# Weight words of the attention stage: one staging buffer against two, and reads one or two slots ahead against three

## The chip, the cores and the metric

The kernel runs on one core of a Trainium2 chip. The metric is the device time of one execution in microseconds (us). Three executions of the kernel before took 984.76, 985.96 and 990.31 us; the median, 985.96, stands for it below.

## The reference

A causal attention with a bias made of running sums (4 batches, 8 heads, 576 positions, 64 wide) is followed by two feed-forward blocks of 2304 tokens, 512 wide inside and 2048 wide in the middle:

```
x = attention(q, k, v, s)                     # 2304 x 512
g = relu(x @ moe_w_in) ** 2                   # 2304 x 2048
y = g @ moe_w_out                             # 2304 x 512
h = y @ moe2_w_in                             # 2304 x 2048
out = max(0.01 * h, h) @ moe2_w_out           # 2304 x 512
```

The four weight matrices arrive as 64-bit words, so the kernel has to read 8 bytes for each weight and build a 32-bit float from the low and the high half.

## The kernel before, in words

**Stages.** The first stage does attention and, in between, the first product of the first block (`up1`). A tail without attention follows, with the last token blocks of `up1`; then come `down`, `up` and `down` again for the other three products. The change lies in the first stage, function `attention`.

**Slots.** Attention runs over 16 pairs of heads, 7 slots each (`n = len(STEPS)`), so `end` is 112. In each slot one row tile of scores is reduced on VectorE (line 438), goes through the exponential on ScalarE (line 462, nine instructions for a pair) and is turned on TensorE two slots later (line 472). The products with `v` are line 508. From slot 39 on `fill` mixes matmuls of `up1` (line 593) into the slots: block `j` of 512 tokens starts behind slot `START[j] = 28 * (j + 1) + 10`, and its 16 groups, one for each chunk of `moe_w_in`, are spread over the 23 slots behind that. Each group ends with a Relu (line 579) and a Square (line 580) on ScalarE.

**Weights in attention.** Sixteen jobs `load_w` make the chunks of `moe_w_in` that `up1` multiplies with, two and a half slots apart from slot `CV` on. Thirteen jobs `convert` (`BEFORE`) make chunks of `moe_w_out`, three slots apart from slot 72 on, and write them to a scratch in HBM (line 180). A job is a generator; `at_slot` says in which slots it goes one step on. One chunk is 128 x 512 words of 64 bits, 512 KB.

- The read is line 153 (`moe_w_in`) or line 151 (`moe_w_out`), on SP's queue, into a tile `wst`.
- `words` builds the floats: line 112 (ScalarE, high words to `wt`), line 116 (VectorE, shift), line 118 or 114 (ScalarE, low words in place), line 120 (the addition: GpSimd for `moe_w_in`, VectorE for `moe_w_out`), line 121 (VectorE, sign; the last use of `wst`).
- `load_w` then splits the result: line 166 (VectorE, copy) and line 167 (GpSimd, subtraction).

Line 112 stands one slot behind the read in `load_w`, two slots behind it in `convert`. `Stage(mx, mx, 1)` gives `wst` one buffer in the pool `mx`, so the read of a chunk waits for line 121 of the chunk before it.

**Other work of GpSimd in a pair:** the low parts of q and k (line 394), small copies of the last rows (line 402), the widened sums (line 531).

**Order.** Each engine runs its instructions in a fixed order. Where a job's step is asked for in a slot, the scheduler of the language still sorts all instructions by when it takes them to be ready, with the program's order as the priority. A change of one dependency can so move many instructions on all engines.

Of the kernel before, what the change touches and what calls it, by code (L numbers as in the profile page):

```python
# [18 lines left out]
def f32(ap):  # L19
    return ap.bitcast(F32)  # L20
# [3 lines left out]
def attention_then_two_mlps(  # L24
# [24 lines left out]
    nc = tc.nc  # L49
# [8 lines left out]
    NR1 = S - R  # L58
    W = 512
    LAG = 2  # L60
    CV = 13
    SB, HN = 768, 384
    ORDER = (1, 7, 6, 2, 5, 4, 3)
    CHAIN = {1: 0, 6: 0, 5: 0, 3: 0, 7: 1, 4: 1, 2: 2}
# [15 lines left out]
    wpool = first.enter_context(tc.tile_pool(name="w", bufs=1))  # L80
# [28 lines left out]
    def words(t, st, adder=nc.gpsimd):  # L109

        lw, hw = st[:, :, 0], st[:, :, 1]
        nc.scalar.activation(f32(t), f32(hw), AF.Copy, scale=2.0 ** -112)  # L112
        if adder is nc.vector:
            nc.scalar.activation(lw, lw, AF.Copy, scale=2.0 ** -29)  # L114
            yield
        nc.vector.tensor_scalar(t, t, 0x07FFFFFF, 3, ALU.bitwise_and, ALU.logical_shift_left)  # L116
        if adder is not nc.vector:
            nc.scalar.activation(lw, lw, AF.Copy, scale=2.0 ** -29)
            yield
        adder.tensor_tensor(t, t, lw, ALU.add)  # L120
        nc.vector.scalar_tensor_tensor(t, hw, 0xC0000000, t, ALU.bitwise_and, ALU.bitwise_or)  # L121
        yield
# [25 lines left out]
    def read_w(st, w, ch, rows, queue=nc.sync):  # L148

        if rows:  # L150
            queue.dma_start(st.rearrange("p f t -> p (f t)"), w.bitcast(U32)[ch * P:(ch + 1) * P, :])
        else:
            queue.dma_start(
                st.rearrange("p (c f) t -> p c (f t)", c=KC),
                w.bitcast(U32)[:, ch * 2 * P:(ch + 1) * 2 * P].rearrange("(c p) f -> p c f", p=P))

    def load_w(fc, pool, stage, lo_engine=nc.gpsimd):

        st = stage.words()
        read_w(st, w1_in, fc, False)  # L160
        yield
        dst = pool.tile([P, 2, DM], F32R, tag=f"w{fc}", name=f"w{fc}")
        win[fc] = dst
        t = stage.word()
        yield from words(t, st)
        nc.vector.tensor_copy(dst[:, 0], f32(t))
        lo_engine.tensor_tensor(dst[:, 1], f32(t), f32(dst[:, 0]), ALU.subtract)
# [3 lines left out]
    def convert(mat, ch, stage, queue=nc.gpsimd, lag=3):  # L171

        w, rows = LATER[mat]
        st = stage.words()
        read_w(st, w, ch, rows, queue)
        for _ in range(lag):
            yield
        t = stage.word()
        yield from words(t, st, nc.vector)
        nc.gpsimd.dma_start(wscr[mat][ch], f32(t))  # L180
# [379 lines left out]
    def up1_x(mp, j, c, bufs):  # L560

        n, w = BLOCKS[j]
        xf = mp.tile([P, w], F32, tag="xf", name="xh", bufs=2)
        nc.sync.dma_start(xf, xscr[c, :, n:n + w])
        yield
        t = mp.tile([P, 2, w], F32R, tag="xs", name="xs", bufs=bufs)
        xs[j, c] = t
        split([t[:, z] for z in range(2)], xf)
# [32 lines left out]
    def attention(at, mg, mx):  # L601
# [5 lines left out]
        def at_slot(y, f, *args):  # L607
            later.setdefault(y, []).append((f, args))
# [52 lines left out]
        def store(x):  # L661
            p = pairs[x]
            for e in range(2):
                c, d0 = divmod(p.h[e] * D, P)
                nc.sync.dma_start(xscr[c, d0:d0 + D, p.b * S:(p.b + 1) * S], p.xo[64 * e:64 * e + 64])

        for fc in range(FC):
            job = load_w(fc, wpool, Stage(mx, mx, 1))
            for gap in range(4):
                at_slot(CV + 5 * fc // 2 + gap, step, job)  # L670
        for ch in range(BEFORE):
            job = convert(0, ch, Stage(mx, mx, 1), nc.sync, 2)
            for gap in (0, 1, 2, 3, 4, 5):
                at_slot(end - 3 * BEFORE - 1 + 3 * ch + gap, step, job)
        START = [4 * n * (j + 1) + 10 for j in range(B)]
        for j in range(B):
            for c in range(KC):
                job = up1_x(mx, j, c, XS)
# [295 lines left out]
    with tc.tile_pool(name="mg", bufs=1) as mg, tc.tile_pool(name="mx", bufs=1) as mx:  # L974
        with tc.tile_pool(name="at", bufs=1) as at:
            attention(at, mg, mx)
        pad, wr = [late.enter_context(tc.tile_pool(name=x, bufs=1, side="right", reuse_waits="tile"))
                   for x in ("pd", "wr")]
        pad.tile([P, 120], F32, tag="pad", name="pad")
        for i in EARLY:  # L980
            wparts[i] = wr
        with tc.tile_pool(name="s3", bufs=1, side="right", reuse_waits="tile") as s3,                 tc.tile_pool(name="s2", bufs=1, side="right", reuse_waits="tile") as s2,                 tc.tile_pool(name="mt", bufs=1, side="right", reuse_waits="tile") as mt:
            stage, other = Stage(s2, s2, 2), Stage(s3, s3, 1)
            for x in range(BEFORE, BEFORE + 7):
                jobs.add(x - BEFORE, convert, *divmod(x, FC), stage, nc.gpsimd, 2)
            for at, q, x in ((0, 0, other), (5, 1, other), (10, 2, other), (12, 3, stage)):
                jobs.add(at, arrive, 0, q, x, EARLY, True)
            for c in range(KC):
                for _ in up1_x(mt, B, c, KC):
                    pass  # L990
            for j in (B - 1, B):
                for _ in up1(mg, j, jobs.tick):
                    pass
            jobs.finish()
# [6 lines left out]
    with ExitStack() as stack:  # L1001
        b = open_pools(stack, ("b10", "bp2", "bp1", "bwst", "b00", "b01", "bop0", "bop1", "b11", "bwt"))
        stage = Stage(b["bwst"], b["bwt"], 2)
# [10 lines left out]
    with ExitStack() as stack:  # L1014
        b = open_pools(stack, ("c62", "cpa", "cpb", "cwst", "c17", "cy", "c543", "cp2", "cwa", "cwt"))
        stage, other = Stage(b["cwst"], b["cwt"], 2), Stage(b["cwa"], b["cwa"], 6)
# [52 lines left out]
```

## Time and profile before

| | |
|---|---|
| median of three executions | 985.96 us |
| the profiled execution | 989.75 us |
| its span, first to last instruction | 986.9 us |
| mean granted clock of TensorE | 0.989 of full speed |
| busy: TensorE, its weight loads | 942.2, 840.5 us |
| busy: VectorE, ScalarE, GpSimd | 691.5, 595.0, 203.0 us |
| DMA moved | 178.5 MB, 181 GB/s |

The span is 2.85 us shorter than the profiled execution's time. In the rows PE is TensorE, PEld its weight loads, DVE VectorE, ACT ScalarE, POOL GpSimd, SPq SP's queue of DMAs, and L112 line 112. Busy shares are means over the whole span, and the stages differ: attention with its `up1` takes about the first 350 us, the tail goes to about 450 us, and the other three products take the rest. Matmuls are pipelined and their ends are modelled, so a busy TensorE is not one at its peak. An idle time is put down to the event that ended it.

### The profile page before, as it was taken

The numbers are of one execution on the slowest core, as the hardware profiler recorded it, in microseconds if no ns is written. First come the engines' busy times: TensorE is split into PE (matmuls) and PEld (weight loads), VectorE is DVE, ScalarE is ACT, GpSimd is POOL, SyncE is SP. The second block draws the span as 40 slices with busy tenths as digits, with TensorE's granted clock in tenths as the row PEclk, the third lists the DMA queues.
The fourth block names the chain that finished last, engine by engine and source line by source line (L and its number), as shares of the span: only waits on it lengthen the run. The fifth ranks groups of instructions, "written<-read, shape, count | busy, mean of one in ns | idle before, by whom it ended". The sixth has DMA issues, their size and how long they took to land.

```text
span 986.9 us, 16713 instructions
## 1 busy us (share of the span) xinstructions
PE 942.2 (95%) x6056; PEld 840.5 (85%) x6056; DVE 691.5 (70%) x1281; ACT 595.0 (60%) x1095; POOL 203.0 (21%) x329
## 2 busy tenths in 40 slices
PE   5998999899999999889999999999999999999998
PEld 4665766677767768789999999999999999999998
DVE  6787667644585534648889799679568788685863
ACT  5775766665667646766566556568567764444442
POOL 5565555422232002100121100101111000000000
PEclk9998999999999999999999999999999999999999
DMA  8774756473754565994856833866868674617201
GB/s 143 142 169 111 183 170 143 128 187 103 204 161 153 172 204 195 323 345 149 273 179 204 295 102 113 258 204 231 319 199 301 206 257 122 183 42 221 75 17 49
DMA packets 191818, 178.50 MB, mean 181 GB/s; under 512 B 101428, under 2 KB 167028, under 8 KB 191736
## 3 DMA queue, kind: packets, MB, share of 16 engines
q1 hardware_dynamic: 153712, 98.35, 36.1%
q0 software_dynamic: 11776, 41.03, 12.2%
q10 hardware_dynamic: 26248, 38.06, 10.5%
q8 instruction: 47, 0.77, 0.3%
q14 instruction: 35, 0.29, 0.1%
HBM read 111.25 MB, written 66.13 MB: 180 GB/s over the span
## 4 chain that ended last, share of the span: by engine, by line
PE 38%; DMA 9%; issue 7%; DVE 6%; ACT 3%; POOL 1%; SPq 0%; ACTq 0%; POOLq 0%; DVEq 0%
PE q L773 36%; DVE op L879 3%; DMA gp<-gscr 2%; DMA wst<-in_moe_w_in_dram 2%; PE h L593 2%; DMA gscr<-gs 1%; DMA wst<-in_moe_w_out_dram 1%; DVE gp L873 1%; DMA xh<-xscr 1%; DMA wb<-wscr 1%; DMA gp<-qscr 1%; ACT r L579 1%; ACT op L878 0%; ACT wst L114 0%; DVE gp L871 0%
## 5 line engine op out<-in xcount | busy, mean ns | idle before, releaser
L773 PE MATMUL q<-op,w 128*128 128x384 f32 x2016 | 354.9, 336 | 7.3 <-DVE op L879 4.7
L773 PEld LDWEIGHTS q<-op,w 128*128 128x128 f32 x2016 | 350.5, 188 | 11.6 <-DVE op L879 6.8
L878 ACT ACTIVATE op<-gp 128x768 fp32r<-128x768 f32 x189 | 158.1, 845 | 160.9 <-PE q L773 138.6
L593 PE MATMUL h<-xs,w 128*128 128x512 f32 (+1 forms) x960 | 224.7, 382 | 6.7 <-ACT r L579 3.7
L879 DVE TENSOR_TENSOR op<-gp,op 128x768 fp32r<-128x768 f32 x189 | 178.1, 955 | 47.5 <-ACT op L878 47.3
L593 PEld LDWEIGHTS h<-xs,w 128*128 128x128 f32 x960 | 162.3, 190 | 43.3 <-ACT r L579 6.5
L773 PE MATMUL q<-w,op 128*128 128x256 f32 x1512 | 182.1, 283 | 1.0 <-DVE op L879 1.0
L773 PEld LDWEIGHTS q<-w,op 128*128 128x128 f32 x1512 | 181.7, 192 | 1.4 <-DVE op L879 1.4
L462 ACT ACTIVATE t<-t,m 128x128 f32<-128x128 f32 (+2 forms) x144 | 83.3, 580 | 43.0 <-DVE m L438 40.9
L438 DVE CUSTOM_DVE_ANT_0 t<-S,mask 128x128 f32<-128x128 f32 (+2 forms) x129 | 57.9, 475 | 39.6 <-PE S L422 22.9
L472 PE MATMUL tr<-ident,t 128*128 128x128 f32 x384 | 68.0, 288 | 11.9 <-ACT t L462 11.1
L180 POOL DMA_DIRECT2D wscr<-wt x48 | 26.7, 556 | 245.2 <-DVE wt L121 231.6
L472 PEld LDWEIGHTS tr<-ident,t 128*128 128x128 f32 x384 | 45.8, 144 | 30.7 <-ACT t L462 14.2
L112 ACT ACTIVATE wt<-wst 128x512 f32<-128x512 f32 x64 | 42.4, 662 | 45.1 <-DMA wst<-in_moe_w_in_dram 24.1
L579 ACT ACTIVATE r<-h 128x512 f32<-128x512 f32 (+1 forms) x80 | 43.6, 547 | 33.2 <-PE h L593 32.6
L848 DVE TENSOR_TENSOR post<-q,post 128x768 f32<-128x768 f32 x54 | 51.6, 955 | 15.2 <-PE q L773 14.8
L508 PE MATMUL tr<-pT,v 128*64 128x320 f32 (+3 forms) x384 | 54.6, 404 | 3.9 <-DVE pT L718 3.8
L116 DVE TENSOR_SCALAR wt<-wt 128x512 uint32<-128x512 uint32 x64 | 30.2, 472 | 39.4 <-ACT wt L112 39.3
L718 DVE COPY pT<-tr 128x384 f32<-128x384 f32 (+2 forms) x80 | 40.4, 521 | 22.9 <-PE tr L472 22.9
L121 DVE SCALAR_TENSOR_TENSOR wt<-wst,wt 128x512 uint32<-128x512 uint32 x64 | 48.5, 757 | 11.0 <-POOL wt L120 10.2
L422 PE MATMUL S<-Y 64*128 64x128 f32 (+3 forms) x354 | 44.3, 358 | 9.4 <-ACT Y L393 9.3
L508 PEld LDWEIGHTS tr<-pT,v 128*64 128x64 f32 x384 | 29.5, 142 | 27.4 <-DVE pT L718 6.7
(103 smaller groups left out, 1025.8 us busy)
## 6 DMA issues: line engine op xcount, KB each, us to landing
gscr<-gs ACTq DMA_DIRECT2D x36, 512.0 KB
gp<-gscr SPq DMA_DIRECT2D x48, 384.0 KB
qscr<-post ACTq DMA_DIRECT2D x48, 384.0 KB
gp<-qscr SPq DMA_DIRECT2D x48, 384.0 KB
wscr<-wt POOLq DMA_DIRECT2D x48, 256.0 KB, 4.5
wst<-in_moe_w_out_dram POOLq DMA_DIRECT2D x19, 512.0 KB, 5.4
wst<-in_moe_w_in_dram SPq DMA_DIRECT2D x16, 512.0 KB
wst<-in_moe_w_in_dram POOLq DMA_DIRECT2D x16, 512.0 KB, 5.6
```

The lines of the kernel that those rows point to most:

```text
L121: nc.vector.scalar_tensor_tensor(t, hw, 0xC0000000, t, ALU.bitwise_and, ALU.bitwise_or)
L422: nc.tensor.matmul(p.sc[kind][e][:, a:z], qs[hs, T * P:(T + 1) * P], ks[hs, :z - a], start=(n == 0 and y == 0), stop=(n == len(tiles) - 1 ...
L438: return nc.vector.tensor_tensor_reduce(t[:, a:z], sc, msk, -QK_SCALE, first, ALU.add, ALU.min, m).ins
L462: done = nc.scalar.activation(t[:, a:z], t[:, a:z], AF.Exp, bias=m[:, c:c + 1], scale=-1.0, accum_out=sums[:, s0:s0 + 1])
L472: nc.tensor.transpose(tr[:, c * P:(c + 1) * P], t[:, c * P:(c + 1) * P], ident)
L508: p.anchor = nc.tensor.matmul(po[64 * e:64 * e + 64, a:n], p.vr[:, c, e], rhs[e], start=(y == 0), stop=(y == len(mm) - 1), skip_group_chec ...
L579: nc.scalar.activation(r[:, :w], h[:, :w], AF.Relu)
L593: nc.tensor.matmul(h[:, :w], win[fc][:, a, c * P:(c + 1) * P], xs[j, c][:, z, :w], start=(c == 0 and y == 0), stop=(c == KC - 1 and y == 2))
L773: i = nc.tensor.matmul(*args, skip_group_check=True, **kw).ins
L848: done = nc.vector.tensor_tensor(t[1], acc, t[1], ALU.add)
L878: a = nc.scalar.activation(t[:, 0], src, AF.Copy)
L879: c = nc.vector.tensor_tensor(t[:, 1], src, f32(t[:, 0]), ALU.subtract)
```

## The change

It alters five things, all in `attention` or the job that it calls.

- `wst` and `wt` of the attention stage move from pool `mx`, which lives on through the tail, to pool `at`, which is freed at the end of attention. `wst` gets two buffers instead of one; `wt` keeps two.
- In `load_w` line 112 stands three slots behind the read instead of one; the job takes six slots instead of four.
- `CV`, the slot of the first read, is 11 instead of 13. The first line 112 stays in slot 14.
- In `convert` as attention uses it line 112 stands three slots behind the read instead of two. The slots of the reads stay, so each conversion comes one slot later.
- `BEFORE` stays 13.

```
-    CV = 13
+    CV = 11
...
         read_w(st, w1_in, fc, False)
-        yield
+        for _ in range(3):
+            yield
         dst = pool.tile([P, 2, DM], F32R, tag=f"w{fc}", name=f"w{fc}")
...
+        stage = Stage(at, at, 2)
         for fc in range(FC):
-            job = load_w(fc, wpool, Stage(mx, mx, 1))
-            for gap in range(4):
+            job = load_w(fc, wpool, stage)
+            for gap in range(6):
                 at_slot(CV + 5 * fc // 2 + gap, step, job)
         for ch in range(BEFORE):
-            job = convert(0, ch, Stage(mx, mx, 1), nc.sync, 2)
-            for gap in (0, 1, 2, 3, 4, 5):
+            job = convert(0, ch, stage, nc.sync, 3)
+            for gap in range(6):
                 at_slot(end - 3 * BEFORE - 1 + 3 * ch + gap, step, job)
```

In the changed kernel the lines behind 161 have numbers that are higher by one, those behind 668 by two.

Two places show what the scheduler makes of it. The first is SP's queue of DMAs in the second pair; `v` and `ag` are the values and the bias rows of a coming pair. Before:

```order
L370 DMA v<-in_v_dram 128x4x64
L382 DMA ag_88<-aug 4x1152 x2
L370 DMA v<-in_v_dram 128x4x64
L372 DMA v<-in_v_dram 64x2x64
L153 DMA wst<-in_moe_w_in_dram 128x4x256
L370 DMA v<-in_v_dram 128x4x64 x2
L372 DMA v<-in_v_dram 64x2x64
L382 DMA ag_90<-aug 4x1152 x2
```

Now:

```order
L153 DMA wst<-in_moe_w_in_dram 128x4x256
L383 DMA ag_88<-aug 4x1152 x2
L371 DMA v<-in_v_dram 128x4x64 x2
L373 DMA v<-in_v_dram 64x2x64
L153 DMA wst<-in_moe_w_in_dram 128x4x256
L371 DMA v<-in_v_dram 128x4x64 x2
L373 DMA v<-in_v_dram 64x2x64
L383 DMA ag_90<-aug 4x1152 x2
```

The read of the first chunk now stands ahead of the bias rows of one pair and the values of another, where the second chunk's read takes its old place.

The second place is VectorE in the third pair, ahead of all `up1` work; `t,m<-S,mask` is the reduction of the scores, `w` a finished chunk. Before:

```order
L121 SCALAR_TENSOR_TENSOR wt<-wst,wt 128x512
L523 TENSOR_SCALAR sums<-sums 128x4
L166 CAST w_569<-wt 128x512
L524 RECIPROCAL sums<-sums 128x4
L438 ISA t,m<-S,mask 128x512
L438 ISA m 128x1
L718 COPY pT_683<-tr 128x3x128
L438 ISA t,m<-S,mask 128x512
```

Now:

```order
L121 SCALAR_TENSOR_TENSOR wt<-wst,wt 128x512
L524 TENSOR_SCALAR sums<-sums 128x4
L116 TENSOR_SCALAR wt<-wt 128x512
L167 CAST w_571<-wt 128x512
L525 RECIPROCAL sums<-sums 128x4
L439 ISA t,m<-S,mask 128x512
L439 ISA m 128x1
L121 SCALAR_TENSOR_TENSOR wt<-wst,wt 128x512
```

One conversion stood between these reductions, two stand there now: line 116 of the next chunk and its line 121 came in between. Over the stage the conversions move up as a whole. Ahead of the 52nd exponential on ScalarE stood six instructions of line 112, now nine; line 112 of the sixteenth chunk stood behind 85 exponentials, now behind 67; and the Square of the sixteenth `up1` group stood behind 90, now behind 79.

## Rows read from the trace of the kernel before

**Rows 1.** The chain that ended last: its first step; start us, us, what.

```profile
354.36 0.02 SPq L665
```

**Rows 2.** Windows: us; busy PE, PEld, DVE, ACT, POOL; PE's clock, DMA share, GB/s.

```profile
75.00:100.00 25.00, 21.76 (x128) 14.50 (x125) 18.95 (x54) 15.22 (x39) 13.20 (x19) 0.86 0.41 108
125.00:150.00 25.00, 24.20 (x157) 17.81 (x157) 15.54 (x45) 17.25 (x41) 13.47 (x17) 1.00 0.50 159
150.00:175.00 25.00, 22.87 (x143) 16.88 (x142) 18.05 (x52) 15.39 (x37) 11.87 (x17) 0.93 0.67 155
175.00:200.00 25.00, 21.72 (x145) 16.43 (x144) 17.31 (x51) 16.19 (x37) 11.46 (x18) 0.93 0.39 114
200.00:225.00 25.00, 25.00 (x142) 18.72 (x141) 10.60 (x32) 17.10 (x41) 5.30 (x11) 1.00 0.76 189
275.00:300.00 25.00, 22.71 (x150) 16.74 (x150) 19.91 (x57) 17.47 (x44) 8.05 (x13) 1.00 0.53 162
```

**Rows 3.** Waits in the first 360 us: total, times, longest.

```profile
ACT wt L112 <- DMA wst<-in_moe_w_in_dram: 19.5, 14, 3.4
ACT wt L112 <- DMA wst<-in_moe_w_out_dram: 14.4, 8, 4.3
DVE wt L121 <- POOL wt L120: 10.2, 8, 1.8
```

**Rows 4.** TensorE's timeline: idle gaps behind a conversion; idle and releaser in brackets.

```profile
52.76 0.66 PE L472 MATMUL tr<-ident,t 128*128 128x128 f32 x4 [1.93 <-ACT t L462]
82.93 1.12 PE L472 MATMUL tr<-ident,t 128*128 128x128 f32 x4 [2.10 <-ACT t L462]
136.19 0.74 PE L593 MATMUL h<-xs,w 128*128 128x512 f32 x2 [0.31 <-DVE w L166]
151.58 0.73 PE L593 MATMUL h<-xs,w 128*128 128x512 f32 x2 [1.14 <-DVE w L166]
179.56 0.33 PE L472 MATMUL tr<-ident,t 128*128 128x128 f32 x1 [2.91 <-ACT t L462]
276.45 0.66 PE L472 MATMUL tr<-ident,t 128*128 128x128 f32 x4 [0.68 <-ACT t L462]
295.15 0.66 PE L472 MATMUL tr<-ident,t 128*128 128x128 f32 x4 [1.60 <-ACT t L462]
```

**Rows 5.** Timeline: a read on SP's queue and three of line 112 that waited for reads.

```profile
75.72 0.40 SPq L153 DMA_DIRECT2D wst<-in_moe_w_in_dram  x1
50.73 0.66 ACT L112 ACTIVATE wt<-wst 128x512 f32<-128x512 f32 x1 [2.46 <-DMA wst<-in_moe_w_in_dram]
80.91 0.66 ACT L112 ACTIVATE wt<-wst 128x512 f32<-128x512 f32 x1 [3.40 <-DMA wst<-in_moe_w_in_dram]
293.18 0.66 ACT L112 ACTIVATE wt<-wst 128x512 f32<-128x512 f32 x1 [4.30 <-DMA wst<-in_moe_w_out_dram]
```

**Rows 6.** Instructions of a conversion: ns min/median/max; last, issue of a read to landing.

```profile
L116 DVE TENSOR_SCALAR wt<-wt x16: 384/428/1596, 38.8 to 185.4; 128x512 uint32<-128x512 uint32 x16
L120 POOL TENSOR_TENSOR wt<-wt,wst x16: 1277/1302/1326, 39.3 to 187.1; 128x512 uint32<-128x512 uint32 x16
L121 DVE SCALAR_TENSOR_TENSOR wt<-wst,wt x15: 642/693/1896, 42.9 to 178.9; 128x512 uint32<-128x512 uint32 x15
L166 DVE CAST w<-wt x15: 385/428/1064, 44.0 to 182.2; 128x512 fp32r<-128x512 f32 x15
L167 POOL TENSOR_TENSOR w<-wt,w x16: 1270/1282/1300, 45.1 to 191.7; 128x512 fp32r<-128x512 f32 x16
DMA to landing us min/median/max: 3.9/5.4/9.0
```

**Rows 7.** Windows, columns as in rows 2: the second and the fourth pair, and pairs two to five.

```profile
24.00:38.00 14.00, 12.08 (x101) 9.00 (x99) 9.81 (x37) 9.79 (x27) 5.54 (x13) 1.00 0.66 150
52.60:65.80 13.20, 12.77 (x93) 8.54 (x93) 11.87 (x40) 9.91 (x30) 9.48 (x17) 0.87 0.49 132
24.00:83.80 59.80, 52.22 (x402) 37.60 (x401) 49.86 (x166) 42.64 (x114) 33.92 (x55) 0.96 0.71 156
```

## Prediction

> **What bounds the kernel now.** I begin with the chain of waits, and it does not help: followed back from the end it reaches only to 354 us [rows 1], so it never enters attention. What it shows of waits for `wst` belongs to the tail, whose staging buffers the change does not touch. Attention has to be read from the windows, the waits and the timeline.
>
> The windows say where TensorE is short of work [rows 2]. From 200 to 225 us it is busy for all 25 us at full clock while VectorE is busy for 10.6: there attention is bound by TensorE, and a wait elsewhere costs nothing. In five other windows it has idle time: 3.24 us (75 to 100), 0.80 (125 to 150), 2.13 (150 to 175), 3.28 (175 to 200) and 2.29 (275 to 300), together 11.74 us. In three of these the granted clock is below 1 as well, 0.86, 0.93 and 0.93. The two levels are 2.4 and 1.2 GHz, so a mean of 0.86 is 28% of 25 us at the lower one, 7 us in which half the work is done: 3.5 us lost. The two windows at 0.93 lose 1.75 us each. Idle time and clock make 18.7 us, which is the most that any repair between 75 and 350 us can return.
>
> The waits name a suspect [rows 3]: line 112, the first step of a conversion, waited for its read 22 times, 33.9 us in all. A read issued at 75.72 us let line 112 start at 80.91, 5.2 us later [rows 5]; the reads of GpSimd's queue took 5.4 us in the median and up to 9.0 [rows 6]. A slot early in attention is 2 us long (14.0 us for a pair of seven slots [rows 7]), so a lead of one slot cannot cover such a read. ScalarE runs in order, hence the exponentials behind line 112 wait too, and TensorE behind them: its gap of 2.10 us at 82.93 stands two us behind the wait of 3.40, the gap of 1.60 at 295.15 behind the wait of 4.30 [rows 4, 5].
>
> **The change part by part.**
>
> *Earlier reads and two buffers.* Three slots are 6 us at 14 us a pair, more than 5.2, though less than the slowest 9.0. The twelve pairs behind the fourth share the time from 65.8 to some 354 us [rows 1, 7], 24 us each, so three slots are some 10 us there, enough for all. I take the waits of rows 3 for reads as gone. What that is worth goes by TensorE alone. Of its gaps between 75 and 350 us six end on an exponential or a weight behind a conversion [rows 4]: 2.10 + 0.31 + 1.14 + 2.91 + 0.68 + 1.60 = 8.74 us, 74% of the 11.74. With the same share of the clock's 7.0 us, 5.2, that is 13.9. Not all of it comes back, since a conversion also waits inside itself, VectorE at line 121 for GpSimd's line 120, 10.2 us in 8 times [rows 3], and nothing takes that away. I keep three quarters: **-10 us**. The bounds are -3.7 (only the two gaps that follow a long read wait directly, 2.10 and 1.60) and -18.7 (all of it).
>
> *Conversions that move up.* The order shows nine of line 112 ahead of the 52nd exponential where six stood. So three conversions leave the stretch that TensorE bounds and enter the one where attention runs almost alone, bound by its own chain. Each brings VectorE 0.43 + 0.69 + 0.43 = 1.55 us at the medians [rows 6], 4.65 for three. A pair with only the start of one conversion took 14.0 us with VectorE busy for 9.81; one with more took 13.2 with 11.87 busy [rows 7]. There is room, but not for all: 1.3 us free in the fuller pair. Against it stands the gap of 1.93 us at 52.76 [rows 4], which goes with the read wait of 2.46 us ahead of it [rows 5]. I take +4.65 - 1.93, about **+3 us**; the bounds are -2 (all fits, the gap goes) and +19 (worked out below, with the slower rival).
>
> *SP's queue.* The first read moves ahead of one pair's `ag` and `v` loads. SP's issue of such a read takes 0.40 us [rows 5], 29 reads as before. A read now waits for the line 121 of two chunks earlier, and it stands one slot behind that step; loads of `q`, `k` and `v` queued behind it wait along, as they did behind the read of one chunk earlier. Nothing added: 0.
>
> *Conversions of `moe_w_out` one slot later, and `wst` in pool `at`.* The scratch writes come a slot later, long before the tail reads them. Taking `wst` out of `mx` moves every tile of `at` down by 8 KB, so the first reads of the tail wait for other tiles of the last pair than before. Last uses in the last pair differ by a slot or so. I take 0; below a shorter wait of one slot, above a longer one, 3.4 us at 24 us a pair, either way.
>
> *Everything resorted.* The scheduler moved instructions on all engines up to the end of attention and a few at the start of the first `down`. The work is the same. I price this at nothing and leave it in the width of the range.
>
> The sum: -10 + 3 = **-7 us**. The profiled execution took 989.75 us, so its counterpart is 982.75. It lies 3.8 us above the median of the three executions, 985.96, and the time that I give is for the median: 985.96 - 7 = **979.0 us**, 0.7% faster. A measurement of this kernel can tell about 0.5% from no change, 4.9 us here: faster is under 981.0, slower over 990.9.
>
> **The rivals.**
>
> *Slower: VectorE and GpSimd cannot carry the conversions where they now stand.* Nine conversions over the 3.7 pairs of exponentials 18 to 51 are 2.4 a pair. VectorE needs 9.81 + 2.4 x 1.55 = 13.5 us for a pair, still under 14.0. But line 121 also waits for GpSimd, 1.3 us a time in rows 3, which makes 16.7; and line 121 has taken 1896 ns where its median is 693 [rows 6], about the length of one GpSimd addition, 1302 ns, longer. If each conversion meets both, a pair takes 19.8 us. Pairs two to five took 59.8 us [rows 7]; at 19.8 they take 79, +19, and with the -10 of later the kernel ends at 985.96 + 9 = 995. It decides where these pairs go over 17.5 us each: 2.5 more than their mean of 15.0, four times, is the gain. For it speaks that GpSimd, busy for 9.48 of 13.2 us in the fuller pair [rows 7], gets 2.58 us more with each conversion; against it, that this fuller pair was quicker than the emptier one.
>
> The Trainium skill has a rule that speaks for this rival (SBUF — State Buffer, section "SBUF: two separate sides"): VectorE and GpSimd share one pair of SBUF ports as an exclusive lock, and a VectorE instruction with two SBUF inputs stands still for the whole of a GpSimd instruction that holds it. The 1896 ns of line 121 agree with that. If by that rule each of the three conversions blocked VectorE for both its GpSimd instructions, the sum would be 7.7 us worse, about 987.
>
> *No change: the read waits were not TensorE's.* Most of the 33.9 us fell where TensorE had work queued. Then only the two direct gaps come back and half of what the clock lost from 75 to 100 us: -3.7 - 1.75, with +3 early about -2.5, 983.5. For it speaks that 33.9 us of such waits on ScalarE stand against 8.74 us of gaps on TensorE [rows 3, 4]; against it, that four of those six gaps end on an exponential, which is what line 112 holds up.
>
> *Faster by more: all of the 18.7 us comes back and the early pairs take the conversions for nothing*, -20 and some 966. It needs every small gap to close.
>
> *It does less than it says.* If the scheduler had left the conversions where they were, the longer lead would be on paper only. The order excludes that: the sixteenth line 112 stands 18 exponentials earlier.
>
> **How the numbers follow.** Forecast -7, with what lies between -13 and -5: 0.50. More, near 966: 0.10. No change near 983.5: 0.25. Slower, near 995: 0.15. The forecast's own tail above 981.0 is small, 0.03. So faster 0.57, same 0.28, slower 0.15. The likeliest case alone spans 973 to 981. The range reaches from 966, the best case, to 992, within the slower rival's start; outside are perhaps 0.05 below and 0.1 above.
>
> **What would show it.** In the changed profile line 112 should have hardly any wait for `wst` in attention, the windows from 75 to 200 us a clock of 1.00 and under 3 us of idle TensorE, and attention should end near 347 us instead of 354. Pairs two to five should take some 3 us more together. The forecast is wrong if these pairs grow by over 10 us, if line 121's waits for GpSimd grow beyond 20 us, if read waits stay because SP issues the reads late, or if attention ends earlier and the tail gives it back.

## The result, and the profile after

Six executions of the changed kernel took 974.63 to 982.88 us, median 977.28; six of the kernel before, on the same chip, 984.76 to 994.67, median 986.79. The ratio is 0.990 with a 95% interval of 0.986 to 0.994: faster by 1.0%, 9.5 us. Forecast were 979.0 us against a median before of 985.96, so -7; the time lies in the range and the sign is the likeliest one. The profiled execution of the changed kernel took 982.88 us, its span 981.0.

Two marks in the timeline say where the gain lies: the last exponential of attention (ScalarE) and the first matmul of the third stage, `down` (TensorE); start us, us, what. In the kernel before:

```profile
347.37 0.78 ACT L462 ACTIVATE t<-t,m 128x576 f32<-128x576 f32 x1
437.55 0.45 PE L773 MATMUL q<-op,w 128*128 128x384 f32 x1 [0.22 <-ACT op L878]
```

In the changed kernel:

```profile
337.79 0.78 ACT L463 ACTIVATE t<-t,m 128x576 f32<-128x576 f32 x1 [0.40 <-DVE m L439]
428.39 0.44 PE L775 MATMUL q<-op,w 128*128 128x384 f32 x1 [0.22 <-ACT op L880]
```

Attention ends 9.6 us earlier, the tail keeps that (90.2 us between the marks before, 90.6 after), and `down` begins 9.2 us earlier. From there to the end of the span it took 549.3 us before and 552.6 after, although the change touches nothing there. That stage took 544.3 to 552.6 us over the 14 profiles of this study, with the change at the top of it. So the difference of two spans (5.9 us) is not the gain; that of the medians (9.5) agrees with the marks (9.2).

Windows of the changed kernel, columns as in rows 2; the last is pairs two to five, which answers to the last of rows 7:

```profile
50.00:75.00 25.00, 20.20 (x158) 13.91 (x160) 24.05 (x73) 18.69 (x50) 17.88 (x24) 1.00 0.69 180
75.00:100.00 25.00, 22.28 (x156) 15.21 (x152) 24.84 (x63) 15.69 (x42) 18.99 (x26) 1.00 0.61 155
100.00:125.00 25.00, 23.50 (x143) 17.82 (x144) 16.19 (x46) 18.26 (x44) 15.85 (x18) 1.00 0.73 185
125.00:150.00 25.00, 25.00 (x155) 18.47 (x154) 17.80 (x49) 18.89 (x45) 16.30 (x21) 1.00 0.69 214
150.00:175.00 25.00, 25.00 (x160) 18.86 (x158) 9.75 (x37) 14.38 (x35) 5.34 (x12) 1.00 0.53 118
175.00:200.00 25.00, 24.96 (x179) 18.48 (x178) 17.21 (x54) 17.36 (x44) 7.21 (x15) 1.00 0.34 103
275.00:300.00 25.00, 25.00 (x166) 18.00 (x164) 20.96 (x56) 19.65 (x48) 10.44 (x14) 1.00 0.45 144
23.40:86.30 62.90, 52.35 (x400) 37.82 (x399) 54.62 (x165) 43.54 (x117) 40.25 (x57) 0.97 0.74 171
```

Pairs two to five take 62.9 us instead of 59.8, 3.1 more. VectorE is busy for 4.76 us more there and has hardly anything free from 50 to 100 us (24.05 and 24.84 of 25). Lines 112 and 166 (now 167) in these pairs; ns min/median/max, first and last start. Before:

```profile
L112 ACT ACTIVATE wt<-wst x5: 659/663/691, 37.1 to 80.9; 128x512 f32<-128x512 f32 x5
L166 DVE CAST w<-wt x4: 418/426/518, 44.0 to 76.9; 128x512 fp32r<-128x512 f32 x4
```

In the changed kernel:

```profile
L112 ACT ACTIVATE wt<-wst x7: 659/662/677, 38.8 to 83.9; 128x512 f32<-128x512 f32 x7
L167 DVE CAST w<-wt x6: 423/542/1691, 46.8 to 79.1; 128x512 fp32r<-128x512 f32 x6
```

So two more conversions stand in these pairs, not three: of the nine ahead of the 52nd exponential two begin in pair six. And VectorE's steps of a conversion ran longer there.

Behind pair five TensorE hardly waits any more: from 125 to 200 us it idles for 0.04 us where it idled for 6.21 [rows 2], 2.29 come back from 275 to 300, and the granted clock is 1.00 in every window where it was 0.86 or 0.93. From the end of pair five to the last exponential the changed kernel takes 337.79 - 86.30 = 251.5 us, before 347.37 - 83.80 = 263.6: -12.1. With the later end of pair five, +2.5 (3.1 longer, begun 0.6 earlier), that is the 9.6.

Waits of the changed kernel in the first 360 us, as in rows 3 (line 118 is the second step of a conversion on ScalarE):

```profile
DVE wt L121 <- POOL wt L120: 6.5, 4, 2.8
ACT wst L118 <- DMA wst<-in_moe_w_in_dram: 5.7, 3, 3.2
ACT wt L112 <- DMA wst<-in_moe_w_in_dram: 4.7, 3, 2.8
```

Waits for a read fell from 33.9 us to 10.4, and those for `moe_w_out` are gone. VectorE's wait for GpSimd fell too, from 10.2 to 6.5 us.

### The profile page after: what moved, and what is told of

Read it like the earlier page. It is cut to its first block, busy times and chain, and to the rows that moved or that the text cites. A ratio compares the mean times of both kernels' runs of the same rounds, so it can differ in the third digit from the quotient of the medians.

```text
span 981.0 us, 16721 instructions
## 1 busy us (share of the span) xinstructions
PE 936.2 (95%) x6056; PEld 836.7 (85%) x6056; DVE 694.9 (71%) x1281; ACT 594.1 (61%) x1095; POOL 206.4 (21%) x329
## 4 chain that ended last, share of the span: by engine, by line
PE 31%; issue 19%; DMA 8%; DVE 3%; ACT 2%; POOL 2%; SPq 0%; ACTq 0%; POOLq 0%; DVEq 0%
PE q L775 29%; PE h L594 2%; DMA wst<-in_moe_w_out_dram 2%; DMA wb<-wscr 2%; DMA gp<-gscr 1%; DVE op L881 1%; DMA wst<-in_moe_w_in_dram 1%; DMA xh<-xscr 1%; POOL wscr L181 1%; POOL zscr L943 1%; DMA qscr<-post 1%; POOL wst L153 1%; DMA sscr<-wb 0%; DMA wb<-sscr 0%; ACT r L580 0%
## 5 line engine op out<-in xcount | busy, mean ns | idle before, releaser
L594 PE MATMUL h<-xs,w 128*128 128x512 f32 (+1 forms) x960 | 228.2, 383 | 4.9 <-ACT r L580 3.6
L850 DVE TENSOR_TENSOR post<-q,post 128x768 f32<-128x768 f32 x54 | 51.6, 955 | 15.2 <-PE q L775 14.8
L395 POOL TENSOR_TENSOR Y<-yt,Y 128x576 fp32r<-128x576 f32 x30 | 45.7, 1534 | 50.8 <-ACT Y L394 50.7
L509 PE MATMUL tr<-pT,v 128*64 128x320 f32 (+3 forms) x384 | 52.0, 396 | 4.0 <-DVE pT L720 4.0
L112 ACT ACTIVATE wt<-wst 128x512 f32<-128x512 f32 x64 | 42.2, 660 | 17.4 <-DMA wst<-in_moe_w_in_dram 10.2
L957 POOL DMA_DIRECT2D out_dram<-post x11 | 8.3, 752 | 203.7 <-DVE post L850 187.8
L832 ACT ACTIVATE post<-q 128x768 f32<-128x768 f32 x54 | 43.5, 806 | 11.4 <-PE q L775 10.2
```

The lines of the kernel that those rows point to most:

```text
L395: (nc.vector if x == 0 else nc.gpsimd).tensor_tensor(lo, yt, f32(hi), ALU.subtract)
L509: p.anchor = nc.tensor.matmul(po[64 * e:64 * e + 64, a:n], p.vr[:, c, e], rhs[e], start=(y == 0), stop=(y == len(mm) - 1), skip_group_chec ...
L594: nc.tensor.matmul(h[:, :w], win[fc][:, a, c * P:(c + 1) * P], xs[j, c][:, z, :w], start=(c == 0 and y == 0), stop=(c == KC - 1 and y == 2))
L850: done = nc.vector.tensor_tensor(t[1], acc, t[1], ALU.add)
```

## The experiments

Every ratio is to the kernel before on the same chip; medians of that one were 986.09 to 988.61 us. Read waits are those of lines 112 and 118 in the first 360 us, in us; the last column is the start of the last exponential, which every kernel's one profile gives.

| kernel | median us | ratio, 95% interval | waits w_in / w_out | pairs 2 to 5 | last exp. |
|---|---|---|---|---|---|
| before | | 1 | 19.5 / 14.4 | 59.8 | 347.4 |
| the change | 977.28 | 0.990 (0.986, 0.994) | 10.4 / 0 | 62.9 | 337.8 |
| e1_in_only | 980.44 | 0.9926 (0.9904, 0.9948) | 5.8 / 15.9 | 66.3 | 343.1 |
| e2_out_only | 984.32 | 0.9957 (0.9930, 0.9983) | 15.0 / 0 | 60.7 | 342.8 |
| e3_buffers_only | 979.70 | 0.9924 (0.9901, 0.9947) | 7.1 / 0 | 63.0 | 338.2 |
| e4_leads_only | 992.01 | 1.0051 (1.0023, 1.0079) | 19.7 / 6.9 | 61.5 | 352.7 |
| e5_place_only | 991.37 | 1.0036 (1.0011, 1.0061) | 17.1 / 16.2 | 60.5 | 348.3 |
| e6_three | 974.49 | 0.9863 (0.9837, 0.9890) | 2.3 / 0 | 64.8 | 336.9 |
| e8_late | 971.62 | 0.9843 (0.9815, 0.9870) | 4.6 / 0.3 | 59.1 | 336.6 |
| e9_early_start | 986.17 | 0.9981 (0.9962, 1.0000) | 24.5 / 15.2 | 66.0 | 350.7 |
| e10_three_late | 976.89 | 0.9893 (0.9846, 0.9940) | 2.4 / 0 | 58.7 | 335.7 |
| e11_late_copy | 973.41 | 0.9874 (0.9830, 0.9917) | 6.2 / 0 | 64.6 | 338.8 |
| e12_late_dense | 970.92 | 0.9840 (0.9800, 0.9881) | 9.6 / 0 | 58.5 | 333.2 |
| e13_old_pace | 979.27 | 0.9909 (0.9875, 0.9944) | 2.2 / 0 | 58.9 | 341.0 |

All ten kernels in which a second or third buffer serves the reads, or a part of them, lie at 0.984 to 0.996, the three with one buffer at 0.998 to 1.005. Each edit also makes the scheduler sort the instructions anew, which by itself moves the time (e5, 0.4%), so two single kernels prove little; the two groups do not overlap.

### Which chunks: e1_in_only and e2_out_only

The first keeps the change for `moe_w_in` alone. Against the changed kernel:

```
-            job = convert(0, ch, stage, nc.sync, 3)
+            job = convert(0, ch, Stage(mx, mx, 1), nc.sync, 2)
```

> The moe_w_in part of the change alone: two buffers in pool at and a lead of three slots for load_w, while convert keeps one buffer in mx and its lead of two slots. Theory (the read waits hold up ScalarE and TensorE): of TensorE's gaps of before 6.46 of 8.74 us and all lowered clock lie in the moe_w_in stretch, so some three quarters of 6.46 + 5.2 come back and pairs two to five cost 3 more: about -6 us, ratio 0.994. Read waits of line 112 for moe_w_out stay near 14 us. Rival (the gain comes from a moved placement or a resorted order, not from reads): nothing to choose between the parts, ratio anywhere, not tied to where read waits go.

The second does the other half. Against the kernel before:

```
+        stage = Stage(at, at, 2)
...
         for ch in range(BEFORE):
-            job = convert(0, ch, Stage(mx, mx, 1), nc.sync, 2)
+            job = convert(0, ch, stage, nc.sync, 3)
```

> The moe_w_out part alone: convert gets two buffers in pool at and a lead of three slots, load_w keeps one buffer in mx and its lead of one slot. Theory: gaps of 0.68 and 1.60 us behind 275 us come back, some -2 us, ratio 0.998, same within 0.5%; pairs two to five take 60 us as before. Rival (placement or order): as large a gain as the whole change, 0.99.

Measured: 0.9926 and 0.9957, together 1.2% where both at once give 1.0%. Each part removes its own reads' waits and leaves the other's. In e1:

```profile
ACT wt L112 <- DMA wst<-in_moe_w_out_dram: 15.9, 10, 4.5
```

In e2:

```profile
ACT wt L112 <- DMA wst<-in_moe_w_in_dram: 15.0, 9, 3.3
```

At the last exponential the two parts gave 4.3 and 4.5 us, together 8.8 of the 9.6. The part with `moe_w_out` is thus no small one, though it was expected to be. Of its 4.5 us, 3.4 came in pairs six to ten, where `moe_w_out` is not yet converted. So these are not from the wait that the edit takes away; the order that the scheduler made anew is what is left.

### The buffer or the lead: e3_buffers_only and e4_leads_only

The first has the buffers and the pool of the change with the leads and the start of before. Against the changed kernel:

```
-    CV = 11
+    CV = 13
...
-        for _ in range(3):
-            yield
+        yield
...
-            job = convert(0, ch, stage, nc.sync, 3)
+            job = convert(0, ch, stage, nc.sync, 2)
```

> Two buffers in pool at, with the old leads (first read in slot 13, one slot ahead of line 112, two for moe_w_out). Theory: a read takes 5.2 us and a slot is 2 to 3.4 us long, so line 112 still waits for most reads, over 20 us in all; no change within 0.5%, ratio 0.996 to 1.002. Rival (the second buffer is what counts, since a read waited for line 121 of the chunk before): as good as the whole change, 0.99.

The second has the leads and the start of the change with one buffer in the old pool:

```
-        stage = Stage(at, at, 2)
+        stage = Stage(mx, mx, 1)
```

> The new leads with one buffer in mx. Theory: a read cannot start ahead of line 121 of the chunk before, so conversions keep the pace of read plus conversion as before, line 112 waits on, and loads behind a read on SP's queue wait longer for it; ratio 0.998 to 1.006. Rival (the lead is what counts): 0.99.

I expected nothing of the buffer alone. It brings the gain, 0.9924 with an interval that overlaps that of the change, and its last exponential comes 0.4 us behind the change's; the longer lead alone costs, 1.0051. SP's queue says why. Reads of `moe_w_in` from 46 us on in the kernel before:

```profile
46.61 0.38 SPq L153 DMA_DIRECT2D wst<-in_moe_w_in_dram  x1
55.32 0.39 SPq L153 DMA_DIRECT2D wst<-in_moe_w_in_dram  x1
64.19 0.42 SPq L153 DMA_DIRECT2D wst<-in_moe_w_in_dram  x1
```

In e4, with three slots of lead:

```profile
47.62 0.39 SPq L153 DMA_DIRECT2D wst<-in_moe_w_in_dram  x1
56.80 0.38 SPq L153 DMA_DIRECT2D wst<-in_moe_w_in_dram  x1
65.63 0.43 SPq L153 DMA_DIRECT2D wst<-in_moe_w_in_dram  x1
```

In the changed kernel:

```profile
47.88 0.69 SPq L153 DMA_DIRECT2D wst<-in_moe_w_in_dram  x1
51.37 0.40 SPq L153 DMA_DIRECT2D wst<-in_moe_w_in_dram  x1
57.86 0.38 SPq L153 DMA_DIRECT2D wst<-in_moe_w_in_dram  x1
65.21 0.40 SPq L153 DMA_DIRECT2D wst<-in_moe_w_in_dram  x1
```

In e3, with one slot of lead:

```profile
48.01 0.68 SPq L153 DMA_DIRECT2D wst<-in_moe_w_in_dram  x1
51.53 0.40 SPq L153 DMA_DIRECT2D wst<-in_moe_w_in_dram  x1
58.06 0.38 SPq L153 DMA_DIRECT2D wst<-in_moe_w_in_dram  x1
65.42 0.40 SPq L153 DMA_DIRECT2D wst<-in_moe_w_in_dram  x1
```

With one buffer a read comes about every 9 us in this stretch whatever lead is written; with two, e3 reads within 0.2 us of the change. It fits that the scheduler takes a read to be ready when its buffer is free and puts it there: the written lead hardly counts. The single buffer also set the pace of the conversions: GpSimd's subtraction, their last step, runs from 45.1 to 191.7 us before [rows 6] and to 193.1 in e4, but to 147.9 in the changed kernel and 147.2 in e3.

Why e4 is slower than before stays open. It waits less for reads (26.6 us), but pairs eleven to sixteen take 150.6 us instead of 146.6.

### The pool alone: e5_place_only

`wst` keeps one buffer and moves to `at` with `wt`. Against the kernel before:

```
-            job = load_w(fc, wpool, Stage(mx, mx, 1))
+            job = load_w(fc, wpool, Stage(at, at, 1))
...
-            job = convert(0, ch, Stage(mx, mx, 1), nc.sync, 2)
+            job = convert(0, ch, Stage(at, at, 1), nc.sync, 2)
```

> A control: wst and wt go to pool at with one buffer for wst, leads and first slot as before. It moves every tile of at by 8 KB and makes the tail's first reads wait for other tiles, and nothing else. Theory (the second buffer is the cause): no change, ratio 0.997 to 1.003, conversions at the pace of before. Rival (placement): part of the gain of 0.99 shows here.

Measured 1.0036: the pool brings nothing, it costs a little. e5 and e3 differ in the second buffer alone, and between them lie 1.1%. The reads' waits in e5 are those of before:

```profile
ACT wt L112 <- DMA wst<-in_moe_w_in_dram: 17.1, 11, 3.6
ACT wt L112 <- DMA wst<-in_moe_w_out_dram: 16.2, 9, 4.7
```

### Waits or earlier weights: e9_early_start and e13_old_pace

Two buffers do two things: they take stalls away and they finish the weights 44 us sooner, so that `up1` can start sooner. The first experiment starts the conversions earlier with one buffer. Against the kernel before:

```
-    CV = 13
+    CV = 5
```

> The kernel before with CV 5 instead of 13: one buffer and every read wait stay, but conversions of moe_w_in begin eight slots earlier, so that at the old pace of one in 9.8 us the sixteenth ends some 16 us earlier. Theory A (stalls: ScalarE waits for a read and holds up the exponentials): the read waits stay near 20 us and the time with them, ratio 0.998 to 1.004. Theory B (pace: one buffer makes a conversion take read plus conversion, so the weights come too late for up1): the weights are there sooner and half of the gain of the moe_w_in part comes, ratio 0.996 or better, with gaps between 150 and 250 us (5.4 before) under 2.

Measured 0.9981, not told from no change. The sixteenth conversion came at 172 us (184 before, 139 in the change), so the buffer held the pace and only part of the cause was tried. Behind pair five e9 takes 261.1 us, 2.5 less than before, but its pairs two to five take 66.0, 6.2 more. In the second pair one read held ScalarE, and the exponentials queued behind it, for 7.33 us:

```profile
31.91 0.66 ACT L112 ACTIVATE wt<-wst 128x512 f32<-128x512 f32 x1 [7.33 <-DMA wst<-in_moe_w_in_dram]
```

The second experiment keeps the two buffers and spreads the conversions, and starts the first two blocks of `up1` eight slots later:

```
-                at_slot(CV + 5 * fc // 2 + gap, step, job)
+                at_slot(CV + 16 * fc // 5 + gap, step, job)
...
-        START = [4 * n * (j + 1) + 10 for j in range(B)]
+        START = [4 * n * (j + 1) + (18 if j < 2 else 10) for j in range(B)]
```

> The changed kernel with its two buffers, but at the late pace of the kernel before: conversions of moe_w_in 3.2 slots apart (the sixteenth behind 80 exponentials; 85 before, 67 in the change), and the first two up1 blocks eight slots later, so that the sixteenth Square stands behind 89 exponentials (90 before, 79 in the change). Theory A (stalls: what gains is that ScalarE no longer waits for reads): read waits are gone here too, so the gain stays, ratio 0.984 to 0.992. Theory B (pace: what gains is that weights and so up1 come earlier and TensorE has work in its gaps): the gain goes, ratio 0.996 to 1.003, and fewer than 210 up1 matmuls lie before 200 us (199 before, 232 in the change).

Measured 0.9909, as good as the change. How much of `up1` (line 593, now 594) ran from 25 to 200 us; us, busy PE and PEld, clock, DMA share, GB/s. Before:

```profile
25.00:200.00 175.00, 56.88 (x199) 36.07 (x199) 0.95 0.60 149
```

In the changed kernel:

```profile
25.00:200.00 175.00, 65.15 (x230) 40.00 (x230) 0.99 0.62 158
```

In e13:

```profile
25.00:200.00 175.00, 55.59 (x206) 37.00 (x206) 0.97 0.64 157
```

Its last exponential and the last steps of its conversions:

```profile
341.04 0.78 ACT L463 ACTIVATE t<-t,m 128x576 f32<-128x576 f32 x1 [0.39 <-DVE m L439]
L168 POOL TENSOR_TENSOR w<-wt,w x16: 1265/1286/1341, 48.7 to 174.7; 128x512 fp32r<-128x512 f32 x16
```

From the end of pair five to the last exponential, columns as in rows 2; before, the changed kernel, e13:

```profile
83.80:347.37 263.57, 255.07 (x1586) 190.31 (x1585) 162.84 (x469) 175.03 (x417) 94.64 (x145) 0.98 0.56 155
86.30:337.79 251.49, 248.65 (x1590) 185.86 (x1589) 160.09 (x467) 173.69 (x416) 91.51 (x142) 1.00 0.57 157
82.50:341.04 258.54, 253.62 (x1595) 190.31 (x1594) 160.66 (x468) 174.50 (x416) 93.73 (x143) 0.99 0.56 156
```

e13 does hardly more `up1` early than the kernel before (206 matmuls against 199), and still attention ends 6.3 us sooner and the time lies outside what theory B gave. So a gain comes without earlier weights. But 6.3 of 9.6 us is not the share of the stalls, because e13's pairs two to five take 58.9 us and the change's 62.9. Behind pair five, where the change gains 12.1 us, e13 gains 5.0, less than half; TensorE's idle time there is 8.50 us before, 4.92 in e13 and 2.84 in the change. The rest is left to the pace. The limits of this: e13's conversions end at 174.7 us, not at 191.7, so the pace is not quite the old one; the later start of two `up1` blocks was not tried alone; and each number comes from one profile.

### More buffers: e6_three and e10_three_late

Three buffers, five slots of lead, and the start two slots earlier; against the changed kernel:

```
-    CV = 11
+    CV = 9
...
-        for _ in range(3):
+        for _ in range(5):
...
-        stage = Stage(at, at, 2)
+        stage = Stage(at, at, 3)
...
-            for gap in range(6):
+            for gap in range(8):
                 at_slot(CV + 5 * fc // 2 + gap, step, job)
```

> The changed kernel with three buffers for wst, and for load_w a lead of five slots and CV 9. Ten us of read waits are left in the changed kernel between 50 and 135 us. Theory A (they still hold up TensorE): they go, and 1 to 3 us with them, ratio 0.987. Theory B (from 50 to 100 us VectorE is busy for 24 to 25 of 25 us, so ScalarE has time to wait): no gain beyond two buffers, ratio 0.989 to 0.992.

e10 is e6 with `CV = 13`.

> Three buffers and a lead of five slots as in e6_three, with conversions of moe_w_in four slots later (CV 13), as in e8_late. Theory (the two gains are apart: fewer conversions where VectorE is full, and the last read waits): ratio 0.982, one or two us under e8_late. Rival (what e6_three gained against the change was scatter between orders): 0.984 to 0.988.

Both leave some 2.4 us of read waits. The ratios are 0.9863 and 0.9893. e6 by itself fits its theory A: its first `down` matmul stands at 426.78 us, 1.6 ahead of the change. e10 does not bear that out: it is not faster than e8, which starts in the same place with two buffers, and its interval (0.9846 to 0.9940) overlaps those of the change and of e8. A third buffer adds nothing that these runs can tell.

### Where the conversions stand: e8_late, e11_late_copy, e12_late_dense

If pairs two to five pay for the conversions that moved up, a later start gives that back. Against the changed kernel:

```
-    CV = 11
+    CV = 15
```

> The changed kernel with CV 15 instead of 11, so each conversion of moe_w_in comes four slots later, with its two buffers. Theory A (conversions that moved up cost pairs two to five some 3 us because VectorE is full there): some 1.5 conversions fewer in those pairs, which take 60 to 61 us instead of 62.9; the rest of attention stays, ratio 0.987. Theory B (up1 wants its weights early, the pace of conversions is what gains): weights come later than wanted, TensorE's gaps between 90 and 250 us grow by 2 us or more, ratio 0.992 or worse.

Measured 0.9843, the change 0.990, with intervals that just overlap. Pairs two to five, columns as in rows 2:

```profile
23.70:82.80 59.10, 52.38 (x403) 38.14 (x402) 49.70 (x162) 43.53 (x116) 33.73 (x56) 0.97 0.73 164
```

VectorE's 54.62 us and GpSimd's 40.25 are back at 49.70 and 33.73, what the kernel before had [rows 7], and the pairs are back at 59.1 us. Six conversions begin there, seven in the change, five before. This fits a price of conversions in that place, and e10 and e12 (58.7 and 58.5 us) fit it too, but their number alone does not set it: e13 begins seven there, as the change does, and takes 58.9 us, and e1, with the same edit of `load_w` as the change, takes 66.3 with a lower clock:

```profile
23.20:89.50 66.30, 55.66 (x399) 40.52 (x398) 53.61 (x165) 43.86 (x117) 39.68 (x57) 0.90 0.73 170
```

At the first `down` matmul e8 stands 2.4 us ahead of the change (425.98 us), while the medians, of different batches, differ by 5.7; what is between these is open.

e11 is e8 with the copy (line 167) moved off VectorE:

```
-        nc.vector.tensor_copy(dst[:, 0], f32(t))
+        nc.scalar.activation(dst[:, 0], f32(t), AF.Copy)
```

> e8_late with line 167, the copy of the rounded weight, on ScalarE instead of VectorE, for all sixteen chunks: VectorE loses 0.43 us for a chunk, ScalarE gains some 0.66. Theory (VectorE, busy for 24 of 25 us from 50 to 75 us, bounds the early pairs): pairs two to five shrink by 1 to 2 us from e8_late's 59.1, ratio 0.983. Rival (the early pairs are bound by their own chain of waits, through ScalarE): pairs two to five grow by 1 to 3 us, ratio 0.986 or more.

It isn't faster than e8 (0.9874), and the early pairs grow:

```profile
23.20:87.80 64.60, 56.13 (x406) 41.96 (x404) 50.12 (x161) 46.62 (x121) 33.48 (x56) 0.89 0.69 155
```

ScalarE has 3.1 us more, VectorE has not less, the pairs take 5.5 us more, and the granted clock is 0.89. ScalarE's chain is no cheaper a place than VectorE. That VectorE's load by itself makes these pairs long is not shown by it.

e12 starts still later and then converts faster:

```
-    CV = 11
+    CV = 22
...
-                at_slot(CV + 5 * fc // 2 + gap, step, job)
+                at_slot(CV + 2 * fc + gap, step, job)
```

> The changed kernel with conversions of moe_w_in from CV 22 on, two slots apart instead of two and a half; the last comes in slot 55 as in e8_late. Pairs two and three are rid of conversions, pairs four to eight hold them more densely. Theory A (conversions cost most where TensorE does not bound): pairs two to five take some 58 us, ratio 0.982. Theory B (a dense run fills VectorE and GpSimd and brings read waits back): pairs four to eight grow, ratio 0.986 or more.

Pairs two to five, and the last exponential:

```profile
23.40:81.90 58.50, 52.02 (x407) 38.51 (x407) 50.32 (x161) 42.45 (x113) 30.76 (x53) 0.97 0.72 158
333.21 0.78 ACT L463 ACTIVATE t<-t,m 128x576 f32<-128x576 f32 x1 [0.40 <-DVE m L439]
```

Measured 0.9840, median 970.92 us, the lowest of all and not told apart from e8. Pairs four to eight did not grow: 106.7 us, as in the change. Attention ends 4.6 us ahead of the change, although three reads are waited for again:

```profile
ACT wt L112 <- DMA wst<-in_moe_w_in_dram: 9.3, 3, 4.5
```

## Why the prediction was right, and where it was not

- **"Earlier reads and two buffers", -10.** Measured -12.1 us behind pair five. The working gave 13.9 and kept three quarters; the discount was too strong. Its ground was that VectorE's wait for GpSimd stays, but that fell as well, 10.2 to 6.5 us. The accounting by TensorE held: behind pair five its idle time fell from 8.50 to 2.84 us and its clock rose from 0.98 to 1.00 of 263.57 us, some 5 us, together about 11 of the 12.1. TensorE idles for 4.26 us from 75 to 200 us, not for under 3: in the two windows up to 125 us it still waits (2.72 and 1.50).
- **The step that failed** is the one under that term: "Three slots are 6 us ..., more than 5.2", the lead as what covers the read. With one buffer the lead covers nothing (e4, slower); with two, one slot does as well as three (e3). The rival "it does less than it says" was set aside because "The order excludes that". The order did show conversions that move, but the second buffer moved them; the order of before and after cannot say which of two edits did it.
- **"Line 112 should have hardly any wait."** Half right: 10.4 us remain, all on `moe_w_in`, six waits of at most 3.2 us.
- **"Conversions that move up", +3.** Measured +3.1, but that the size came out was luck in part. The working took three conversions into pairs two to five from a count that reaches into pair six; two more stand there, 3.10 us of VectorE at the medians of rows 6. VectorE's extra 4.76 us come near the 4.65 of the working only because steps ran longer, the copies 542 ns in the median instead of 426. The gap of 1.93 us that was taken off did not lower TensorE's idle time in these pairs, which rose from 7.58 us [rows 7] to 10.55. A later start gives the 3.1 us back (e8), though e13 does without one.
- **The slower rival** began where a pair takes over 17.5 us. These pairs took 15.7 on average. Its price of 19 us took every conversion to meet both stalls; line 121 of the changed kernel (ns min/median/max) seldom runs long:

```profile
L121 DVE SCALAR_TENSOR_TENSOR wt<-wst,wt x16: 650/689/1898, 44.6 to 145.1; 128x512 uint32<-128x512 uint32 x16
```

  The Trainium skill's lock between VectorE and GpSimd (SBUF — State Buffer, section "SBUF: two separate sides") agrees with the 1898 ns, but the median of 689 is the old one; the 987 us that it gave when each conversion is blocked did not come.
- **The no-change rival** fell: e13 takes the read waits away with hardly more early `up1`, and its time is 0.9909. How much of the gain was these waits and how much the pace stays open within the limits said above.
- **"`wst` in pool `at`" and "everything resorted", 0 each.** The tail was right (90.2 and 90.6 us). The stage was not: e5, which moves `wst` and `wt` and nothing else, is 0.4% slower, and e2 gained 3.4 us in pairs that its edit does not reach. Such terms are of the size of the forecast and belonged in the width with a number.
- **The end of attention**: forecast 7 us earlier, measured 9.6. The sum was short by 2.1 us for the discount and by 0.5 early, since pair two began 0.6 us sooner.

## What to carry to other kernels

Where a scheduler puts a load as soon as its buffer is free, the number of buffers sets how early a read goes and how fast the work behind it runs, not the lead that is written; count how far apart the reads stand on the queue before lengthening a lead. Put the work that such a buffer sets free where the bounding engine has a backlog: the same two buffers gave 0.990 with a start in slot 11 and 0.984 with one in slot 15 or 22, and `down` began 2.4 and 4.4 us earlier; the intervals of the ratios still touch. Judge a change in one stage by marks at the end of that stage: a stage that no edit touched took 544 to 553 us from profile to profile.

## What was not expected

- A longer lead on a single buffer made the kernel slower, 1.0051, with fewer read waits than before; so did the single buffer's other pool, 1.0036. In both, pairs eleven to sixteen grew by 4 us (150.6 and 150.5 against 146.6). The cause is open.
- Three buffers took the read waits down to 2.3 us, and the time did not follow: e12 waits for 9.6 us and ends attention 3.7 us before e6.
- One 512 KB read early in attention was waited for 7.33 us (e9), when 4.30 was the longest before [rows 5].
